# Half of the first product of batches 3 and 5 by Strassen's algorithm, with q^T, x and v in single buffers

## The chip, the cores and the metric

One core of a Trainium2 chip runs the whole kernel. Its engines work side by side, each through a queue of its own in program order: TensorE (PE, with its weight loads listed as PEld), VectorE (DVE), ScalarE (ACT), GpSimd (POOL) and SyncE (SP, which issues most DMAs). The metric is device time in microseconds for one execution, lower is better.

## The reference

Eight batches; each goes through attention with a linear kernel and then through a mixer with two matrix products (S = 576 tokens, model width 512, hidden width 2048):

```python
q_p, k_p = phi(q), phi(k)              # relu(x)*cos(pos), relu(x)*sin(pos): 64 -> 128 features
kv  = einsum('bhsf,bhsd->bhfd', k_p, v);  z = sum_s k_p
x   = (q_p @ kv) / (q_p @ z + 1e-6)    # heads side by side: [8, 576, 512]
u   = x + (x^T @ U @ V)^T              # low rank, 32
out = u + relu(u @ w_ch1) @ w_ch2      # 512 -> 2048 -> 512
```

Inputs and output are float32; the kernel multiplies in bf16 and sums in float32.

## The kernel before

**Tokens.** 512 of a batch's 576 tokens are four chunks of 128; the last 64 (the tail) of two batches of a pair make one more tile of 128 tokens.

**Slots.** The mixer's matmuls are laid out by hand as one list of units, the slots (`lay_all`, line 1029). In order: batch 0 first product (slots 0 to 15) and second (16 to 31); batch 1 first (32 to 47), tails of the pair (`g1_tail`, gt, four slots), second product (14 slots, 52 to 65), `g2_tail` (4); batch 2 first (70 to 85) and second (86 to 99); batch 3 first (100 to 115), gt (116 to 119), second (120 to 133), g2_tail (134 to 137); batch 4 first (138 to 153), second (154 to 167); batch 5 first (168 to 183), gt (184 to 187), second (188 to 201); batch 6 first (202 to 217), second (218 to 231); batch 7 first (`LAST`, 19 slots), second, and the last tails. After each slot's matmuls come the things put beside that slot: `starts[b]` is the first slot of batch b's first product. Every engine gets its instructions in exactly this order (`manual_schedule`), so an instruction that waits holds everything behind it on its engine.

**First product.** `g1_main(b, j)` (line 661) makes one of 16 chunks of the hidden layer: four matmuls of 512 columns into one of three PSUM banks with the tag g (G3), then a relu on ACT into `hid`. For batch 7 alone, `g1_part(b, m, part)` (line 587) does it by Strassen's algorithm in the form with seven products: a group m of four chunks, parts 1 to 7, each four matmuls of 256 columns. It takes sums and differences of blocks of w_ch1 (`w1_form`, line 557, into `sa`) and of u^T (`uT_form`, line 575, into `tb`), made on VectorE. Parts 1, 6, 5, 3 add up in one bank (al), each read by ACT before the next is added: three casts into `pw`/`py`, one relu. Parts 2 and 7 open banks (be), part 4 adds to 7's; for each, VectorE adds (line 637) and takes the relu (line 634).

**Second product.** From batch 1 on, `w_part(b, n)` (line 819) does it by the same algorithm: seven steps of two slots each, with differences of hid from `hid_form` (S, line 806; half 0 beside the first product, half 1 beside the second) and of w_ch2 (T). Step 0 goes to bank T, steps 1 to 3 open the three banks g, steps 4 to 6 add to these. ACT casts step 0 into `w_sum`; VectorE adds step 1 to it; POOL makes three adds from it (o_sb, line 850); VectorE makes the other adds of line 850. `store` writes o_sb.

**Attention beside it.** `attention_plan(b)` (line 1054) puts batch b's attention beside the products of the two batches before: features `q_prep`, `k_prep` (line 295 on ACT, 297 on VectorE), casts of v by POOL (`v_prep`), transposes by DMA from SP (`qtr_dma`), then `kv_pair` (line 344; 40 matmuls into bank X, the cast on VectorE), five `x_unit` (line 418; eight matmuls, then add, reciprocal and multiply on VectorE: lines 415, 416, 435), `A_unit` (line 457), `u_va` (line 464), `u_add` (line 484), `u_tail`, and u's transposes by DMA (`utr_dma`). The x_units take banks O and X in turns, each of two PSUM banks. `split_o` (line 261) turns O into two single banks, oA and oB, for batch 7's first product.

Of the kernel before, what the change touches and what calls it, by code (L numbers as in the profile page):

```python
# [17 lines left out]
def kernel(  # L18
# [13 lines left out]
    B = 8  # L32
# [150 lines left out]
    v_ext = [const.tile([P, 5, H, E], BF16, name=f"v_ext{i}") for i in range(2)]  # L183
# [8 lines left out]
    v_tl = const.tile([P, H, E], BF16)  # L192
    V_.memset(v_tl[:, :, D:E], 1.0)
    for i in range(2):
        V_.memset(v_ext[i][:, 0:4, :, D:E], 1.0)
# [15 lines left out]
    V_nat = const.tile([R, S], BF16)  # L211
    four = const.tile([R, P], BF16)
# [3 lines left out]
    for i in range(2):  # L216
        G_.memset(v_ext[i][:, 4, :, :], 0.0)
        G_.memset(v_ext[i][tail(i), 4, :, D:E], 1.0)
# [60 lines left out]

    def v_prep(b, h0=0, h1=H, cs=range(5), engs=None):  # L280
        vx = v_ext[b % 2]
        for n, c in enumerate(cs):
            eng = engs[n] if engs else G_
            if eng is None:
                continue
            if c < 4:
                cast(eng, vx[:, c, h0:h1, 0:D], vst[:, h0:h1, c, :])
            elif b < 2:
                cast(eng, v_tl[:, h0:h1, 0:D], vst[:, h0:h1, 4, :])
            else:  # L290
                cast(eng, vx[tail(b), 4, h0:h1, 0:D], vst[tail(b), h0:h1, 4, :])
# [31 lines left out]
    def kv_unit(b, hg, tag, bufs, eng=None):  # L323
        if b not in kv_sb:
            kv_sb[b] = pool.tile([P, H, E], BF16, tag="kv", bufs=2, name="kv")
        n = D if b == 0 else E
        acc = bank([P, 4, n], FP32, tag, bufs, "kv_ps")
        vx = v_ext[b % 2]
        for i in range(4):
            h = hg * 4 + i  # L330
            for c in range(5):
                nc.tensor.matmul(  # L332
                    out=acc[:, i, :],
                    lhsT=k_p[b][:, c, h, :] if c < 4 else k_tl[:, h, :],
                    rhs=(
                        v0[:, h, c, :] if b == 0
                        else v_tl[:, h, :] if c == 4 and b < 2 else vx[:, c, h, :]
                    ),
                    start=(c == 0),
                    stop=(c == 4),  # L340
                )
        cast(eng or V_, kv_sb[b][:, hg * 4 : hg * 4 + 4, 0:n], acc)

    def kv_pair(b, tag, bufs):
        kv_sb[b] = pool.tile([P, H, E], BF16, tag="kv", bufs=2, name="kv")
        acc = bank([P, 2, 512], FP32, tag, bufs, "kv_ps")
        vx = v_ext[b % 2]
        for h in range(H):
            g, i = divmod(h, 4)
            for c in range(5):  # L350
                nc.tensor.matmul(  # L351
                    out=acc[:, g, i * E : i * E + E],
                    lhsT=k_p[b][:, c, h, :] if c < 4 else k_tl[:, h, :],
                    rhs=vx[:, c, h, :], start=(c == 0), stop=(c == 4),
                )
# [108 lines left out]
    def u_va(b, *parts):  # L464
# [3 lines left out]
        for d0, tag, bufs in parts:  # L468
            t = bank([P, 2, 512], FP32, tag, bufs, "va_ps")
            for i in range(2):  # L470
                va[d0 + i] = t[:, i, :]
            va[d0, "pair"] = t
        for c in range(4):
            for d0, _, _ in parts:
# [6 lines left out]
        for d0, _, _ in parts:  # L481
            va_ps[b, d0] = va[d0, "pair"]

    def u_add(b, d0):
        nc.vector.tensor_tensor(  # L485
            out=u_bf[b][:, d0 : d0 + 2],
            in0=x_bf[b].rearrange("p c (d n) -> p d c n", n=P)[:, d0 : d0 + 2],
            in1=va_ps[b, d0].rearrange("p d (c n) -> p d c n", n=P), op=ALU.add,
        )
# [85 lines left out]
    def uT_form(b, n, tag):  # L575
        if b not in tb:
            tb[b] = pool.tile([P, 4, 2, 256], BF16, tag=tag, bufs=1, name="tb")
# [9 lines left out]
    def g1_part(b, m, part):  # L587
        if b not in hid:
            hid[b] = pool.tile([P, NJ, 512], BF16, tag="hid", bufs=1, name="hid")
        if b not in pw:  # L590
            pw[b] = (
                pool.tile([P, 4, 512], FP32, tag="k_p", bufs=1, name="pw"),
                pool.tile([P, 2, 512], FP32, tag="q_p", bufs=1, name="py"),
            )
        ks = slice(2 * m, 2 * m + 2)
        hf, k0 = divmod(2 * m, 4)

        def s_of(n):
            return sa[hf][:, n, :, k0 : k0 + 2, :]
# [17 lines left out]
        for k_ in range(2):  # L617
# [6 lines left out]
        e = m % 2  # L624
        p_, w_, y_ = (
            t_.rearrange("p (k n) -> p k n", k=2)
            for t_ in (pw[b][0][:, 2 * e], pw[b][0][:, 2 * e + 1], pw[b][1][:, e])
# [56 lines left out]
    def g1_tail(pr, jq):  # L684
        if pr not in hid_tl:
            tag, bufs = ("q_pT", 2) if pr == NPAIR - 1 else ("hid_tl", 1)
# [60 lines left out]
    def g2_tail(pr, part):  # L747
        if part == 0:
            o_ps[pr] = bank([P, DM], FP32, *T1, "ot_ps")
# [15 lines left out]

    HD = DM // 2
# [122 lines left out]
    def tl_form(n):  # L889
        if "s" not in tl:  # L890
            tl["s"] = pool.tile([P, 4, KB, P], BF16, tag="q_pT", bufs=2, name="s_tl")
# [19 lines left out]
    def tl_part(step):  # L911
# [12 lines left out]
        if opens:  # L924
            if step == 0:
                tl["o"] = pool.tile([P, 2, DM], FP32, tag="x_bf", bufs=2, name="o_t2")
# [121 lines left out]

    QORD = (4, 0, 1, 2, 3)
# [4 lines left out]
    def attention_plan(b):  # L1054
# [22 lines left out]
        else:  # L1077
# [14 lines left out]
            kv_at, a_at = X0, x_at[4] + 2  # L1092
            u_at = a_at + 1
            a_bank = T1
# [13 lines left out]
        if odd:  # L1108
            put(u_at + 1, u_tail, *T1)
# [277 lines left out]
```

## Time and profile before

| | us |
|---|---|
| runs | 293.81, 294.84, 294.84 (median 294.84) |
| the profiled execution, its own time | 294.04 |
| its span, first to last instruction | 292.2 |
| TensorE busy | 285.7 (98%) |
| VectorE, ScalarE, GpSimd busy | 209.2, 158.1, 74.1 |
| batch 2 second product | 112.8 to 125.1 |
| batch 3 first product | 125.1 to 142.3 |
| batch 5 first product | 191.5 to 208.7 |
| batch 5 second product | 212.3 to 226 |
| batch 7 first product | 254.6 to 270.5 |

In a row of a timeline stand the start, the length, the engine, the line, the operation, output and inputs, shapes and count, and in brackets how long the engine stood idle before it and what ended that. In the chain, a row is start, length, engine, output, line and count. A matmul is shown with its way through the array, so rows overlap; what one costs is read from the start of one to the start of the next.

### The profile page before, as it was taken

Reading aid. Unit: us, or ns where it says so; the run is one execution under the profiler, and the core shown is the slowest. Engines: PE = TensorE matmul, PEld = TensorE weight load, DVE = VectorE, ACT = ScalarE, POOL = GpSimd, SP = SyncE. Lnnn points to the kernel's source line nnn. Section 1 sums busy time; section 2 is a strip of 40 time slices with the busy share of each in tenths; the row PEclk is TensorE's granted clock in tenths of the full one; section 3 lists DMA queues with packets and bytes.
Section 4 is the critical chain, followed back from the end, with each engine's and each line's share of the span. In section 5 each row is a group of like instructions: output and inputs, shape, how many; then the busy total and the mean of one; then the engine's idle time right before and its main releaser. Section 6 shows DMA issues by size and latency. Waiting matters only on the chain.

```text
span 292.2 us, 7236 instructions
## 1 busy us (share of the span) xinstructions
PE 285.7 (98%) x2990; PEld 201.1 (69%) x3018; DVE 209.2 (72%) x406; ACT 158.1 (54%) x274; POOL 74.1 (25%) x111
## 2 busy tenths in 40 slices
PE   8999999999999999999999999999999999999995
PEld 6776455545987546865787546865698548899884
DVE  4889748887894568747744477547779587969884
ACT  2855651575593466845694356936693552067100
POOL 8350600040053304650042500550033002400220
PEclk9999999999999999999999999999999999999999
DMA  6999999999999997699998916999292304030023
GB/s 196 356 247 252 276 205 263 279 172 166 287 225 155 249 350 156 183 260 217 279 201 187 353 54 128 223 238 298 42 152 52 136 6 86 12 134 4 2 84 132
DMA packets 85444, 53.31 MB, mean 182 GB/s; under 512 B 53988, under 2 KB 83076, under 8 KB 85412
## 3 DMA queue, kind: packets, MB, share of 16 engines
q1 hardware_dynamic: 78996, 41.62, 61.9%
q0 software_dynamic: 6272, 11.17, 15.5%
q8 instruction: 23, 0.38, 0.5%
q14 instruction: 9, 0.07, 0.1%
q10 hardware_dynamic: 144, 0.07, 0.1%
HBM read 36.86 MB, written 9.44 MB: 158 GB/s over the span
## 4 chain that ended last, share of the span: by engine, by line
PE 94%; DMA 3%; DVE 1%; issue 1%; ACT 0%; DVEq 0%; ACTq 0%
PE g_ps L671 33%; PE w_ps L838 29%; PE gt_ps L692 5%; PE o_ps L732 5%; PE x_ps L425 3%; DMA kst<-in_k_dram 3%; PE kv_ps L351 3%; PE al_ps L619 2%; PE ot_ps L752 2%; PE ot_ps L939 2%; PE be_ps L619 2%; PE a_ps L451 1%; PE va_ps L476 1%; PE kv_ps L332 1%; PE t_ps L368 1%
## 5 line engine op out<-in xcount | busy, mean ns | idle before, releaser
L671 PE MATMUL g_ps<-uT,w_bf 128*128 128x512 bf16 x428 | 105.5, 380 | 1.0
L680 ACT ACTIVATE hid<-g_ps 128x512 bf16<-128x512 f32 x112 | 66.5, 597 | 69.3 <-PE g_ps L671 44.2
L671 PEld LDWEIGHTS <-w_bf 128*128 128x128 bf16 x448 | 40.1, 98 | 41.4 <-issue 0.2
L850 POOL TENSOR_TENSOR o_sb<-w_sum,u_bf 128x512 f32<-128x512 f32 x21 | 28.3, 1373 | 122.8 <-DVE w_sum L850 122.8
L838 PEld LDWEIGHTS <-hid 128*128 128x128 bf16 x448 | 43.6, 98 | 5.6
L838 PEld LDWEIGHTS <-S 128*128 128x128 bf16 x336 | 32.6, 98 | 4.0
L838 PE MATMUL w_ps<-T,hid 128*128 128x256 bf16 x224 | 26.9, 273 | 0.0
L838 PE MATMUL w_ps<-w_bf,hid 128*128 128x256 bf16 x224 | 26.9, 273 | 0.0
L850 DVE TENSOR_TENSOR o_sb<-o_sb,w_ps 128x512 f32<-128x512 f32 x28 | 19.1, 683 | 9.8 <-PE w_ps L838 5.2
L838 PE MATMUL w_ps<-T,S 128*128 128x256 bf16 x224 | 25.9, 273 | 0.0
L485 DVE TENSOR_TENSOR u_bf<-x_bf,va_ps 128x1024 bf16<-128x1024 bf16 x16 | 19.3, 1217 | 7.2 <-PE va_ps L476 7.2
L116 POOL CAST v_ext<-vst 128x512 bf16<-128x512 f32 (+1 forms) x30 | 18.9, 667 | 14.1 <-DMA vst<-in_v_dram 13.7
L415 DVE TENSOR_SCALAR rec<-x_ps 128x8 f32<-128x8 f32 (+1 forms) x35 | 5.8, 164 | 20.0 <-PE x_ps L425 19.9
L435 DVE TENSOR_TENSOR x_bf<-x_ps,rec 128x512 bf16<-128x512 f32 x28 | 19.4, 692 | 1.0
L295 ACT ACTIVATE k_p<-kst,sinw 128x512 bf16<-128x512 f32 x26 | 17.1, 711 | 0.7 <-DMA kst<-in_k_dram 0.7
L706 POOL DMA_DIRECT2D out_dram<-o_sb x12 | 7.6, 631 | 38.7 <-DVE o_sb L740 21.8
L692 PE MATMUL gt_ps<-uT_tl,w_bf 128*128 128x128 bf16 x256 | 15.8, 219 | 0.0
L692 PEld LDWEIGHTS <-w_bf 128*128 128x128 bf16 x256 | 14.9, 98 | 0.8
L732 PE MATMUL o_ps<-w_bf,hid 128*128 128x512 bf16 x61 | 15.3, 380 | 0.2
L116 DVE CAST kv<-kv_ps 128x520 bf16<-128x520 f32 (+1 forms) x8 | 5.1, 632 | 14.1 <-PE kv_ps L351 9.0
L425 PEld LDWEIGHTS <-q_pT 128*128 128x128 bf16 x224 | 10.8, 98 | 5.9
L295 ACT ACTIVATE q_p<-qst,cosw 128x512 bf16<-128x512 f32 x21 | 14.4, 711 | 0.1
(187 smaller groups left out, 431.7 us busy)
## 6 DMA issues: line engine op xcount, KB each, us to landing
qst<-in_q_dram SPq DMA_DIRECT2D x14, 512.0 KB, 6.4
kst<-in_k_dram SPq DMA_DIRECT2D x14, 512.0 KB, 8.7
vst<-in_v_dram SPq DMA_DIRECT2D x12, 512.0 KB, 8.1
out_dram<-o_sb POOLq DMA_DIRECT2D x12, 512.0 KB, 6.7
w_bf<-in_moe_w_ch_dram POOLq DMA_DIRECT2D x8, 512.0 KB, 10.0
out_dram<-o_sb SPq DMA_DIRECT2D x4, 512.0 KB, 3.0
qst<-in_q_dram SPq DMA_DIRECT2D x2, 640.0 KB
kst<-in_k_dram SPq DMA_DIRECT2D x2, 640.0 KB, 11.0
```

Of the source, the lines that this page charges most:

```text
L116: eng.tensor_copy(out=o, in_=i)
L295: nc.scalar.activation(out=o, in_=i, func=AF.Relu, bias=0.0, scale=w)
L425: nc.tensor.matmul(out=acc[:, g, i * E : i * E + E], lhsT=qT_of(b, c, h), rhs=kv_sb[b][:, h, :], start=True, stop=True,)
L435: nc.vector.tensor_tensor(out=x_of(b, c, rows).rearrange("p (g i d) -> p g i d", g=2, d=D), in0=view[:, :, :, 0:D], in1=rec[rows].unsqueez ...
L485: nc.vector.tensor_tensor(out=u_bf[b][:, d0 : d0 + 2], in0=x_bf[b].rearrange("p c (d n) -> p d c n", n=P)[:, d0 : d0 + 2], in1=va_ps[b, d0 ...
L619: nc.tensor.matmul(out=res[:, k_, :], lhsT=lhs[:, d, k_, :], rhs=rhs[:, d, :], start=(opens and k_ == 0 and d == 0), stop=(k_ == 1 and d = ...
L671: nc.tensor.matmul(out=g_ps.rearrange("p (c t) -> p c t", c=4), lhsT=w1_bf[:, d, j * P : j * P + P], rhs=uT[b][:, d, :, :], start=(d == 0) ...
L680: nc.scalar.activation(out=hid[b][:, j, :], in_=g_ps, func=AF.Relu, bias=0.0, scale=1.0)
L692: nc.tensor.matmul(out=g_ps[:, jj, :], lhsT=w1_bf[:, d, j * P : j * P + P], rhs=uT_tl[pr][:, d, :], start=(d == 0), stop=(d == 3),)
L732: nc.tensor.matmul(out=o, lhsT=hid[0][:, j, cc * P : cc * P + P], rhs=w2_bf[:, j, :], start=(j == 0), stop=(j == NJ - 1),)
L838: nc.tensor.matmul(out=res[:, g, :], lhsT=lhs[:, k_, g * P : g * P + P], rhs=rhs[:, k_, :], start=(opens and k_ == 0 and g == 0), stop=(k_ ...
L850: eng.tensor_tensor(out=o, in0=x, in1=y, op=ALU.add)
```

## The change

Batches 3 and 5 (`MIXED`) do groups 0 and 2 of the four by Strassen's algorithm, their parts laid between the whole chunks of groups 1 and 3 (`HALF`; s4 is chunk 4m + 4). Group m = 0 takes slots 0 to 7 of the stage, m = 2 slots 8 to 15. The banks: al in T, part 2 in g, part 7 in oA.

The sums of w_ch1 for groups 0 and 2 move from batch 5's second product to batch 2's, in a buffer of their own (`sa`); those for groups 1 and 3 stay in batch 6's; each operation covers one group (512 elements, two operations in place of one of 1024). The four `uT_form` of batches 3 and 5 come beside the last four slots before their first products. `split_o` moves from batch 6's end to slot 98, so from batch 4 on the x_units have X alone, A_unit takes oB, u_va takes X and oA, oB (with u_add in three pieces), and u_tail takes half of X two slots later. Batches 4 and 6 get kv_pair one slot later and x_units at slots 5, 8, 13, 16, 18 of the stage in place of 3, 5, 7, 9, 11; their u follows. The first halves of hid_form in batches 3 and 5 move from slots 8 to 11 to slots 9, 11, 17, 18. From batch 4 on ACT makes kv's cast. q_pT, x_bf and the four main chunks of v are held once, not twice; several tiles take other tags. On SP, the tail's q transpose of batch 7 goes ahead of u's first transpose of batch 6, and u^T's second half of batches 5 and 7 ahead of the tail's by more.

```diff
@@ v and its tails
-    v_ext = [const.tile([P, 5, H, E], BF16, name=f"v_ext{i}") for i in range(2)]
+    v_ext = const.tile([P, 4, H, E], BF16)
+    v_ext_tl = [const.tile([P, H, E], BF16, name=f"v_ext_tl{i}") for i in range(2)]
...
@@ kv_pair
         cast(
-            V_, kv_sb[b].rearrange("p (g i) e -> p g (i e)", g=2), acc[:, :, 0 : 4 * E]
+            A_ if b > 3 else V_, kv_sb[b].rearrange("p (g i) e -> p g (i e)", g=2),
+            acc[:, :, 0 : 4 * E],
         )
...
-            q_pT[b] = pool.tile([P, 4, H, P], BF16, tag="q_pT", bufs=2, name="q_pT")
+            q_pT[b] = pool.tile([P, 4, H, P], BF16, tag="q_pT", bufs=1, name="q_pT")
...
-            x_bf[b] = pool.tile([P, 4, DM], BF16, tag="x_bf", bufs=2, name="x_bf")
+            x_bf[b] = pool.tile([P, 4, DM], BF16, tag="x_bf", bufs=1, name="x_bf")
...
@@ w1_form
-    def w1_form(n, hf, tag):
-        if hf not in sa:
-            sa[hf] = pool.tile([P, 4, 2, 4, P], BF16, tag=tag, bufs=1, name=f"sa{hf}")
-        t = sa[hf]
-        ks = slice(4 * hf, 4 * hf + 4)
+    def w1_form(n, m):
+        if m % 2 not in sa:
+            tag = ("sa", "qst")[m % 2]
+            sa[m % 2] = pool.tile([P, 2, 4, 2, 2, P], BF16, tag=tag, bufs=1, name="sa")
+        t = sa[m % 2][:, m // 2]
+        ks = slice(2 * m, 2 * m + 2)
...
@@ g1_part
         if part == 1:
-            g_al[b, m] = bank([P, DM], FP32, *(OA, OB, T1)[m % 3], "al_ps")
+            g_al[b, m] = bank([P, DM], FP32, *((OA, OB, T1)[m % 3] if last else T1), "al_ps")
         elif part in (2, 7):
-            g_be[b, m, part] = bank([P, DM], FP32, *(X1S if part == 2 else G3), "be_ps")
+            tg = (X1S, G3) if last else (G3, OA)
+            g_be[b, m, part] = bank([P, DM], FP32, *tg[part == 7], "be_ps")
...
+    MIXED = {3: (0, 2), 5: (0, 2)}
...
+    HALF = ("1", "s4", "6 2", "s5", "5 7", "s6", "3", "s7 4")
+
     def first_units(b):
         starts[b] = len(slots)
-        lay([lambda j=j: g1_main(b, j) for j in range(NJ)], False)
+
+        def unit(names, m):
+            def go():
+                for n in names:
+                    if n[0] == "s":
+                        g1_main(b, 4 * m + int(n[1]))
+                    else:
+                        g1_part(b, m, int(n))
+
+            return go
+
+        for m in (0, 2):
+            if m in MIXED.get(b, ()):
+                lay([unit(n.split(), m) for n in HALF], False)
+            else:
+                lay([lambda j=j: g1_main(b, j) for j in range(4 * m, 4 * m + 8)], False)
         for i in range(4 * (0 < b)):
-            beside.setdefault(starts[b] + (12 + 2 * i if b == 1 else 8 + i), []).append(
+            n = 12 + 2 * i if b == 1 else (9, 11, 17, 18)[i] if b in MIXED else 8 + i
+            beside.setdefault(starts[b] + n, []).append(
                 lambda i=i: hid_form(b, (1, 2, 4, 3)[i], 0)
             )
...
@@ attention_plan
-            kv_at, a_at = X0, x_at[4] + 2
+            kv_at = X0
+            if b in (4, 6):
+                kv_at, x_at = G + 1, [G + i for i in (5, 8, 13, 16, 18)]
...
+            a_at = x_at[4] + 2
             u_at = a_at + 1
-            a_bank = T1
+            a_bank = T1 if b == 3 else OB
...
-            put(x_at[n], x_unit, c, *(O1, X1)[n % 2])
+            put(x_at[n], x_unit, c, *((O1, X1)[n % 2] if b < 4 else X1))
         put(a_at, A_unit, *a_bank, A_)
-        put(u_at, u_va, (0, *X1), (2, *O1))
+        put(u_at, u_va, (0, *X1), (2, *O1) if b < 4 else (2, OA, OB))
...
-            put(u_at + 1, u_tail, *T1)
+            put(*((u_at + 1, u_tail, *T1) if b < 4 else (u_at + 3, u_tail, *X1S)))
...
-        put(starts[B - 3] + 21 + 2 * n, lambda n=n: w1_form(n, 0, "vst"))
-        put(s6 + 17 + 2 * n, lambda n=n: w1_form(n, 1, "qst"))
-        put(s6 + 24 + n, lambda n=n: uT_form(B - 1, n, "kst"))
+        for m in (0, 2):
+            put(starts[2] + 17 + 2 * n, lambda n=n, m=m: w1_form(n, m))
+            put(s6 + 17 + 2 * n, lambda n=n, m=m: w1_form(n, m + 1))
+        for b in MIXED:
+            put(starts[b] - 4 + n, lambda b=b, n=n: uT_form(b, n))
+        put(s6 + 24 + n, lambda n=n: uT_form(B - 1, n))
...
-    put(s6 + 24, split_o)
+    put(starts[3] - 2, split_o)
```

More of the change, by code (lines that the diff above doesn't have):

```diff
@@ L191 @@
     A_sb = [const.tile([P, P], BF16, name=f"A_sb{i}") for i in range(3)]
-    v_tl = const.tile([P, H, E], BF16)
+    v_tl = pool.tile([P, H, E], BF16, tag="w_sum", bufs=1, name="v_tl")
     V_.memset(v_tl[:, :, D:E], 1.0)
-    for i in range(2):
-        V_.memset(v_ext[i][:, 0:4, :, D:E], 1.0)
+    V_.memset(v_ext[:, :, :, D:E], 1.0)
     V_.memset(q_tlT, 0.0)
@@ L216 @@
     for i in range(2):
-        G_.memset(v_ext[i][:, 4, :, :], 0.0)
-        G_.memset(v_ext[i][tail(i), 4, :, D:E], 1.0)
+        G_.memset(v_ext_tl[i], 0.0)
+        G_.memset(v_ext_tl[i][tail(i), :, D:E], 1.0)
     def cast_uv():
@@ L467, in u_va @@
         va = {}
-        for d0, tag, bufs in parts:
-            t = bank([P, 2, 512], FP32, tag, bufs, "va_ps")
+        for d0, *tags in parts:
+            if tags[0] in (OA, OB):
+                t = [bank([P, 512], FP32, *tg, "va_ps") for tg in tags]
+                va[d0, "pair"] = [x[:, None, :] for x in t]
+            else:
+                x = bank([P, 2, 512], FP32, *tags, "va_ps")
+                t = [x[:, i, :] for i in range(2)]
+                va[d0, "pair"] = [x]
             for i in range(2):
-                va[d0 + i] = t[:, i, :]
-            va[d0, "pair"] = t
+                va[d0 + i] = t[i]
         for c in range(4):
-            for d0, _, _ in parts:
+            for d0, *_ in parts:
                 for d in (d0, d0 + 1):
@@ L480, in u_va @@
                     )
-        for d0, _, _ in parts:
+        for d0, *_ in parts:
             va_ps[b, d0] = va[d0, "pair"]
     def u_add(b, d0):
[L485 to L489, printed above, removed]
+        for t in va_ps[b, d0]:
+            n = t.shape[1]
+            nc.vector.tensor_tensor(
+                out=u_bf[b][:, d0 : d0 + n],
+                in0=x_bf[b].rearrange("p c (d n) -> p d c n", n=P)[:, d0 : d0 + n],
+                in1=t.rearrange("p d (c n) -> p d c n", n=P), op=ALU.add,
+            )
+            d0 += n
     def u_tail(b, tag, bufs):
@@ L623, in g1_part @@
                 )
-        e = m % 2
         p_, w_, y_ = (
-            t_.rearrange("p (k n) -> p k n", k=2)
-            for t_ in (pw[b][0][:, 2 * e], pw[b][0][:, 2 * e + 1], pw[b][1][:, e])
+            pw[b][m % 2 if last else 0][:, i].rearrange("p (k n) -> p k n", k=2)
+            for i in range(3)
         )
@@ L685, in g1_tail @@
         if pr not in hid_tl:
-            tag, bufs = ("q_pT", 2) if pr == NPAIR - 1 else ("hid_tl", 1)
+            tag, bufs = ("kst", 1) if pr == NPAIR - 1 else ("hid_tl", 1)
             hid_tl[pr] = pool.tile([P, NJ, P], BF16, tag=tag, bufs=bufs, name="hid_tl")
@@ L1047 @@
     lay_all()
+    ODDX = (5, 8, 11, 13, 15)
     QORD = (4, 0, 1, 2, 3)
```

47 lines of the change are left out of this document (24 added, 23 removed).

## The prediction

> **What bounds the kernel now.** Four views, in this order. The page's busy rows come first:
>
> ```profile
> PE 285.7 (98%) x2990; PEld 201.1 (69%) x3018; DVE 209.2 (72%) x406; ACT 158.1 (54%) x274; POOL 74.1 (25%) x111
> PEclk9999999999999999999999999999999999999999
> PE 94%; DMA 3%; DVE 1%; issue 1%; ACT 0%; DVEq 0%; ACTq 0%
> ```
>
> TensorE is busy 98% of the span at a full granted clock and is 94% of the chain that ended last. The waits of TensorE alone are two, 1.2 and 0.3 us, both in the first 13 us. So a matmul taken out is worth its own time, and any wait put in front of TensorE is paid in full. Next, what a matmul costs, from the chain in order of time:
>
> ```profile
> 97.46 1.73 PE g_ps L671 x8
> ...
> 259.50 1.31 PE al_ps L619 x12
> ```
>
> A 512-column matmul of a whole chunk advances TensorE by 0.216 us, a 256-column matmul of a Strassen part by 0.109 us, its weight load included. Third, how full VectorE is, stage by stage, from the table of windows (columns: window, length, then PE, PEld, DVE, ACT, POOL):
>
> ```profile
> 96.30:112.80 16.50, 16.40 (x149) 8.10 (x149) 11.38 (x23) 9.12 (x16) 3.00 (x5) 1.00 1.03 299
> 112.80:125.10 12.30, 12.30 (x114) 10.86 (x112) 9.72 (x16) 9.76 (x16) 8.20 (x8) 1.00 0.68 153
> 125.10:142.30 17.20, 16.99 (x179) 9.18 (x182) 9.90 (x22) 9.12 (x16) 3.52 (x6) 1.00 1.04 243
> ```
>
> These are batch 2's first product, batch 2's second product, batch 3's first product. In the middle one VectorE works 9.7 of 12.3 us and POOL, at 8.2 us, is busier than anywhere else. Last, VectorE's timeline there:
>
> ```profile
> 114.22 0.99 DVE L806 TENSOR_TENSOR S<-S,hid 128x1024 bf16<-128x1024 bf16 x1
> 115.14 0.83 DVE L297 TENSOR_SCALAR q_tl<-qst,sinw 64x512 bf16<-64x512 f32 x1
> 115.89 0.82 DVE L297 TENSOR_SCALAR q_p<-qst,sinw 128x512 bf16<-128x512 f32 x1
> ...
> 118.05 0.67 DVE L850 TENSOR_TENSOR w_sum<-w_sum,w_ps 128x512 f32<-128x512 f32 x1
> 118.64 0.67 DVE L806 TENSOR_TENSOR S<-hid,S 128x1024 bf16<-128x1024 bf16 x1
> 120.37 1.48 DVE L850 TENSOR_TENSOR o_sb<-o_sb,w_ps 128x512 f32<-128x512 f32 x2 [1.05 <-POOL o_sb L850]
> ...
> 124.03 0.88 DVE L297 TENSOR_SCALAR k_p<-kst,cosw 128x512 bf16<-128x512 f32 x2
> ```
>
> The last k_p ends at 124.91, and kv_pair of batch 4, which needs it, starts on TensorE at 125.76: 0.85 us of slack. An operation whose operands all lie in SBUF stretches while POOL works: 0.99 for 0.69, 0.83 for 0.48. Batch 6 shows it plainly, VectorE's row first and POOL's (line 850, alone 1.12 to 1.16) after it:
>
> ```profile
> 217.13 1.65 DVE L806 TENSOR_TENSOR S<-hid,S 128x1024 bf16<-128x1024 bf16 x1
> ...
> 216.69 1.53 POOL L850 TENSOR_TENSOR o_sb<-w_sum,u_bf 128x512 f32<-128x512 f32 x1 [20.46 <-DVE w_sum L850]
> ```
>
> S waits until POOL's add ends at 218.2 and then runs some 0.55 us: the two take turns. The adds that read PSUM (w_sum, o_sb) keep 0.67 to 0.69 beside POOL.
>
> **The change, part by part.** *Saved on TensorE.* A group of four chunks costs 16 x 0.216 = 3.46 us whole and 28 x 0.109 = 3.06 us in seven parts; four groups save 4 x 0.40 = 1.6 us. No other matmul goes.
>
> *VectorE in batch 2's second product.* Eight w1_form operations on 512 elements come in, two after each of slots 87, 89, 91, 93, and the four uT_form of batch 3 after slots 96 to 99, each ahead of the k_p feature of its slot. A row for 512 bf16 elements is tb at 0.415 us, 0.34 from start to start (252.88 to 253.21). Other steps from start to start: a form of S 0.60, a feature 0.40, an add 0.60. I walk the new queue from 115.89, where the first pair follows q_tl. While POOL casts v (114.06 to 117.85) each turn is shared: the pair ends at 117.5, then q_p 117.9, the hid form 118.5, q_p 118.9, w_sum 119.5 (before 118.7). Now come pair, S, add, pair, add, pair, add, tb, k_p, add, tb, k_p, tb, k_p: 3 x 0.68 + 0.60 + 4 x 0.60 + 3 x 0.34 + 3 x 0.40 = 7.3 us without POOL, so 126.8. But w_sum releases POOL's three adds, 3 x 1.1 us, in that very stretch; taking turns costs 1.8 us if VectorE goes first whenever two of its operations follow each other, 2.4 us if POOL does (in the rows after 115.2 POOL went first three times of four). The last k_p ends at 128.6 to 129.2.
>
> TensorE wants kv_pair(4) one slot later than before: 124.89 (first matmul of the stage) + 0.44 (part 1) + 0.86 (chunk 4) = 126.2. The wait is 2.4 to 3.0 us; I take 2.8. A part of it shows earlier: part 1 needs bank T, which the third add of the walk releases near 126, 1 us after 124.9. Bounds: 0 if no operation meets POOL (the whole queue then ends at 125.1, from 113.50 by the same steps), 0.6 if only the casts are met, 3.5 if each turn is lost. Behind the wait nothing else is late: VectorE has 10.6 us of work in the 15 us of batch 3's first product (six adds of 0.68, six relus of 0.29, three x_units of 1.1, two S), and catches up.
>
> *Batch 5's end.* Features of batch 7 on VectorE (slots 184 to 186), two S forms and x_units of batch 6 (184, 186) now meet in the four gt slots, 3.6 us + 2 x 0.25. From the last part's end: add and relu 1.05, x_unit to 2.4, feature 2.8, S 3.4, feature 3.8, hid 4.4, x_unit 5.5. A_unit's last four matmuls want that x at 4.06 + 0.87 + 0.31 = 5.25: 0.3 us of wait. Bounds 0 and 1.1 (POOL in the way once). At batch 3 there are no features in those slots: x at 4.7, no wait.
>
> *At nothing, and what covers it.* (1) ACT: three casts and a relu of 0.60 take the place of four relus of 0.60 per group; part 6 follows part 1 by 0.87 us or more while the cast takes 0.2 + 0.60, a margin near zero without the x_unit or kv_pair that lies there (0.25, 1.2 us); if it goes, under 0.1 us a time. (2) kv casts from VectorE to ACT: 0.6 us, ACT idle after its features (2.78 us idle at 126.0). (3) Bank X alone for x_units: one is held 1.6 us (matmuls at 97.04, multiply done 98.63) and the next comes after 1.98; cover 0.4 us, and a late VectorE operation would cost its excess. (4) Single q_pT, x_bf and v_ext: each writer comes after its last reader in slot order, the closest being q_pT of batch 7 (slot 189 after 186). (5) SP: uT of batch 6 is issued behind the q_pT transposes of batch 7 (1.6 to 2.2 us each) at 12.9 us after the last part, lands 4.3 later (median of its rows; 6.8 at most) at 17.2, wanted at 18.6 to 19.0; cover 1.8, cost 0.7 at worst. The tail's uT moves two slots later and is wanted 12 slots on. (6) w1_form in batch 6's second product: eight of 0.34 for four of 0.60, and POOL's turns make VectorE some 1.9 us later at 254.7; there it stood idle 2.5 us until 259.35 (wait of hid for py), which absorbs it. (7) u_add in three pieces: 0.1 us. (8) One memset less, at a start that waits 8.75 us for kst.
>
> *Sum.* -1.6 + 2.8 + 0.3 = +1.5 us. The profiled execution took 294.04 us (span 292.2), so 295.5. The three shown runs are 293.81 and twice 294.84; the profiled execution is 0.8 under their median, and I carry half of that: 296.0.
>
> **A rule against the change.** Weight loads per group rise from 16 to 28 at 98 ns each. In the last batch, where the whole product is in parts, 112 such matmuls advance by 0.109 us each with PEld busy 14.59 of 15.90 us, so the loads hide. Exposed, the 48 extra loads of the four groups would cost 4.7 us. The Trainium skill (TensorE: Matmul & The Clock Gate, The mechanism) says that weight loads overlap running matmuls only when they use other rows of the array, which these do not; by it the sum would be +6.2 us. The trace does not bear it out in the last batch, so the sum goes by the row.
>
> **The rivals.** *Faster: VectorE's backlog never reaches TensorE.* For it: the queue without POOL ends at 125.1, a microsecond before the need, and S at 118.64 kept 0.67 us because it began ahead of POOL's add. Against it: eight new operations just where w_sum lets POOL go. It decides when the last k_p is done by 126.2. Then 294.04 - 1.6 + 0 to 0.3, some 292.6, and 293.0 with the carry; a wait of 0.6 gives 293.6.
> *Slower still: the crowding at batch 5's end also holds TensorE.* POOL once in the way (1.1), uT late (0.7), banks X waiting for VectorE (0.4 each at two or three units): 1 to 2.5 us more, 297 to 298.5. For it: all margins there are under 2 us. Against it: the same stage had 1.79 us of VectorE idle and loses four w1_form of 0.69 to 1.05.
> *The halved matmuls save nothing:* if the weight loads do not hide where whole chunks alternate with parts, 48 x 0.098 = 4.7 us come on top: 300.7. For it: PEld is already at 69%. Against it: the last batch's 0.109 us. The page named above would have it so.
>
> **How the numbers follow.** Forecast 0.52, slower still 0.22, faster rival 0.22 (half of it a partial wait that leaves no measurable gain), nothing saved 0.02, others 0.02 (half on each side). About 0.5%, 1.5 us, is what a measurement can tell from no change. The forecast's own range, 0.9 to 2.0 us over its base, lies across that border, so it is split: 0.28 same, 0.24 slower. Same: 0.28 + 0.11 = 0.39. Slower: 0.24 + 0.22 + 0.02 + 0.01 = 0.49. Faster: 0.11 + 0.01 = 0.12. The forecast's own range is 295.2 to 296.8; the range for 8 in 10 runs from the faster rival with a small wait, 293.2, to slower still, 298.0.
>
> **What would show each step.** In the changed profile: the parts of batches 3 and 5 (line 619 before) advancing 0.109 us a matmul; a TensorE wait of about 1 us before the first al_ps of batch 3, ended by VectorE's o_sb, and one of about 1.7 before kv_ps, ended by VectorE's k_p; w_sum of batch 2 near 119.5 and the last k_p near 129; sa at 0.42 when POOL is idle and near 1 when not. At batch 5's end a 0.3 us wait of a_ps for x_bf. The chain should show DVE at 2% where it had 1%. No wait before kv_ps means the faster rival; waits before va_ps, x_ps or batch 6's g_ps mean the slower one.

## The result, and the profile after

The changed kernel takes 295.57 us (median of 16 runs, 294.84 to 296.78) where the kernel before, run beside it, took 294.31 us (16 runs, 293.54 to 296.36): a ratio of 1.004, 95% interval 1.0023 to 1.0057. It is slower by 1.3 us as the medians stand (0.7 to 1.7 by the interval), about what the forecast of 296.0 had (+1.5 over the profiled execution). The profiled execution of the changed kernel took 294.84 us (span 293.0), the fastest of its runs, so the traces differ by 0.8 us only. 0.25 us of that gap lies at the start: batch 1's tails begin at 73.75 us here and at 74.00 before. The start varies by more than this between kernels that share its code (73.5 to 75.2 us in the traces below), so the stages are compared by their lengths. From batch 1's tails to the first `tl_part` the kernel before takes 208.55 us and the changed one 209.59: +1.04 us, inside the interval.

The page's busy rows and the head of its chain:

```profile
PE 285.0 (97%) x3040; PEld 206.1 (70%) x3066; DVE 219.5 (75%) x445; ACT 160.1 (55%) x278; POOL 73.4 (25%) x111
PE 91%; DVE 3%; issue 3%; POOL 2%; ACT 0%; DVEq 0%; POOLq 0%
```

TensorE's share of the chain falls from 94% to 91%; VectorE and POOL, which had 1% and none, have 3% and 2%. More than half of POOL's share is its casts of v (2.65 us), which the chain reaches through 2.98 us of "issue"; TensorE waits for none of them directly. The waits of TensorE say where (us in total, times, longest):

```profile
PE w_ps L202 <- DVE zero L125: 1.2, 1, 1.2
PE kv_ps L350 <- DVE k_p L301: 0.7, 2, 0.5
PE w_ps L848 <- DVE o_sb L860: 0.7, 1, 0.7
PE a_ps L451 <- DVE x_bf L435: 0.4, 1, 0.4
```

The first is that of the start, as before. The other three are new: before kv_pair, before a step of the second product, and before A_unit's last matmuls. These rows count the idle time alone; what TensorE loses is read from start to start. Its timeline shows the places:

```profile
119.55 1.91 PE L848 MATMUL w_ps<-w_bf,hid 128*128 128x256 bf16 x16
121.59 1.91 PE L848 MATMUL w_ps<-w_bf,S 128*128 128x256 bf16 x16
124.17 1.91 PE L848 MATMUL w_ps<-T,hid 128*128 128x256 bf16 x16 [0.67 <-DVE o_sb L860]
125.91 0.60 PE L629 MATMUL al_ps<-uT,w_bf 128*128 128x256 bf16 x4
...
127.59 0.19 PE L350 MATMUL kv_ps<-v_ext,k_p 128*128 128x65 bf16 x1 [0.16 <-DVE k_p L301]
128.32 0.19 PE L350 MATMUL kv_ps<-v_ext,k_p 128*128 128x65 bf16 x1 [0.54 <-DVE k_p L301]
...
146.98 0.24 PE L451 MATMUL a_ps<-x_tl,U_bf 128*32 128x128 bf16 x4
...
147.38 1.05 PE L848 MATMUL w_ps<-w_bf,hid 128*128 128x256 bf16 x8
...
212.62 0.24 PE L451 MATMUL a_ps<-x_tl,U_bf 128*32 128x128 bf16 x4
...
213.38 0.24 PE L451 MATMUL a_ps<-x_bf,U_bf 128*32 128x128 bf16 x4 [0.35 <-DVE x_bf L435]
213.56 1.05 PE L848 MATMUL w_ps<-w_bf,hid 128*128 128x256 bf16 x8
```

A step of 16 matmuls goes on after 1.75 us when nothing holds it. Step 5 starts 2.04 us after step 4, and step 6 starts 2.58 us after step 5; step 6 writes the bank of step 3, which VectorE reads in the add that ends at 124.12. Step 5's 0.29 us too much are the same kind of wait: it writes the bank of step 2, read by the add that ends at 121.54. So TensorE is held before the stage ends, and not at bank T, where the forecast put it. Bank T came free at 125.38, in time for part 1 at 125.91 only because steps 5 and 6 had been held: without them part 1 was due at 124.80. A_unit (from 212.62) takes 0.94 us to the next step's matmuls in batch 5, where it takes 0.40 in batch 3 (146.98 to 147.38): its wait costs 0.54 us.

VectorE's timeline of the changed kernel in this stretch:

```profile
114.13 0.98 DVE L816 TENSOR_TENSOR S<-S,hid 128x1024 bf16<-128x1024 bf16 x1
...
115.79 0.74 DVE L577 TENSOR_TENSOR sa<-w_bf 128x512 bf16<-128x512 bf16 x2
...
117.84 0.68 DVE L860 TENSOR_TENSOR w_sum<-w_sum,w_ps 128x512 f32<-128x512 f32 x1
118.44 0.75 DVE L577 TENSOR_TENSOR sa<-sa,w_bf 128x512 bf16<-128x512 bf16 x2
119.11 0.68 DVE L816 TENSOR_TENSOR S<-hid,S 128x1024 bf16<-128x1024 bf16 x1
120.85 0.69 DVE L860 TENSOR_TENSOR o_sb<-o_sb,w_ps 128x512 f32<-128x512 f32 x1 [1.06 <-POOL o_sb L860]
121.45 2.06 DVE L577 TENSOR_TENSOR sa<-w_bf 128x512 bf16<-128x512 bf16 x2
123.44 0.68 DVE L860 TENSOR_TENSOR o_sb<-o_sb,w_ps 128x512 f32<-128x512 f32 x1
124.04 0.75 DVE L577 TENSOR_TENSOR sa<-w_bf,sa 128x512 bf16<-128x512 bf16 x2
...
127.70 0.47 DVE L301 TENSOR_SCALAR k_p<-kst,cosw 128x512 bf16<-128x512 f32 x1
```

And POOL's, the three adds that it makes from w_sum in one row; behind it the first of the three as the chain has it:

```profile
118.61 4.63 POOL L860 TENSOR_TENSOR o_sb<-w_sum,u_bf 128x512 f32<-128x512 f32 x3 [3.02 <-DVE w_sum L860]
```

```profile
118.61 2.22 POOL o_sb L860
```

A pair of forms takes 0.75 us, except the one at 121.45, which takes 2.06: it lies beside POOL's adds until 123.24. The add behind it, which frees step 3's bank, comes that much later. The pair at 118.44 and S at 119.11 kept their time, and there POOL paid: its first add took 2.22 us, alone 1.12 to 1.16, and VectorE's next add stood idle for it. The queue's last k_p ends at 128.17; before it ended at 124.91.

The account by stage, from one stage's first matmul to the next one's:

| stage | before | after | difference | what it holds |
|---|---|---|---|---|
| batch 2 second product | 12.22 | 13.49 | +1.27 | waits for o_sb +1.13; steps 1 and 2 +0.14 |
| batch 3 first product | 17.26 | 16.02 | -1.24 | parts -0.80; x_units -0.51 and A_unit with u_va -0.93, moved out; wait for k_p +1.0 |
| its gt, and second product | 15.80 | 17.25 | +1.45 | x_units +0.52, A_unit with u_va +0.93 |
| batch 5 first product | 17.25 | 15.01 | -2.24 | as at batch 3, without a wait |
| its gt, and second product | 17.19 | 19.00 | +1.81 | as at batch 3, A_unit's wait +0.54, and -0.18 at batch 7's kv_pair, which took 1.39 before and takes 1.20 |

From batch 1's tails on, the other stages agree within 0.03 us. Saved are 1.60 us at the parts and 0.18 at kv_pair, lost 1.27 + 1.0 + 0.54 = 2.81: +1.03 us.

### The profile page after: what moved, and what is told of

Its sections match the earlier page's. It is cut to its first block, busy times and chain, and to the rows that moved or that the text cites. A ratio compares the mean times of both kernels' runs of the same rounds, so it can differ in the third digit from the quotient of the medians.

```text
span 293.0 us, 7400 instructions
## 1 busy us (share of the span) xinstructions
PE 285.0 (97%) x3040; PEld 206.1 (70%) x3066; DVE 219.5 (75%) x445; ACT 160.1 (55%) x278; POOL 73.4 (25%) x111
## 3 DMA queue, kind: packets, MB, share of 16 engines
q0 software_dynamic: 6272, 11.17, 15.8%
## 4 chain that ended last, share of the span: by engine, by line
PE 91%; DVE 3%; issue 3%; POOL 2%; ACT 0%; DVEq 0%; POOLq 0%
PE g_ps L680 28%; PE w_ps L848 25%; PE o_ps L741 5%; PE al_ps L629 5%; PE gt_ps L701 4%; PE be_ps L629 4%; PE w_ps L202 3%; PE x_ps L425 3%; PE kv_ps L350 2%; PE ot_ps L761 2%; PE ot_ps L949 2%; PE a_ps L451 1%; PE va_ps L481 1%; POOL v_ext L116 1%; PE kv_ps L335 1%
## 5 line engine op out<-in xcount | busy, mean ns | idle before, releaser
L680 PE MATMUL g_ps<-uT,w_bf 128*128 128x512 bf16 x366 | 90.7, 379 | 0.8
L689 ACT ACTIVATE hid<-g_ps 128x512 bf16<-128x512 f32 x96 | 57.0, 597 | 47.1 <-PE g_ps L680 38.7
L680 PEld LDWEIGHTS <-w_bf 128*128 128x128 bf16 x384 | 34.8, 98 | 34.3 <-issue 0.2
L114 ACT ACTIVATE pw<-al_ps 128x512 f32<-128x512 f32 x24 | 14.2, 596 | 19.4 <-PE al_ps L629 18.7
L646 DVE TENSOR_TENSOR hid<-pw,be_ps 128x512 bf16<-128x512 f32 x24 | 16.4, 684 | 10.5 <-PE be_ps L629 5.8
L492 DVE TENSOR_TENSOR u_bf<-x_bf,va_ps 128x1024 bf16<-128x1024 bf16 (+1 forms) x20 | 19.6, 1003 | 4.2 <-PE va_ps L481 4.2
L701 PE MATMUL gt_ps<-uT_tl,w_bf 128*128 128x128 bf16 x256 | 16.4, 219 | 0.0
L116 POOL CAST v_ext<-vst 128x512 bf16<-128x512 f32 x24 | 15.6, 691 | 2.4 <-DMA vst<-in_v_dram 2.1
L701 PEld LDWEIGHTS <-w_bf 128*128 128x128 bf16 x256 | 15.0, 98 | 0.4
```

What stands on the lines that cost most here:

```text
L116: eng.tensor_copy(out=o, in_=i)
L492: nc.vector.tensor_tensor(out=u_bf[b][:, d0 : d0 + n], in0=x_bf[b].rearrange("p c (d n) -> p d c n", n=P)[:, d0 : d0 + n], in1=t.rearrange ...
L646: V_.tensor_tensor(out=o, in0=x, in1=res, op=ALU.add)
L680: nc.tensor.matmul(out=g_ps.rearrange("p (c t) -> p c t", c=4), lhsT=w1_bf[:, d, j * P : j * P + P], rhs=uT[b][:, d, :, :], start=(d == 0) ...
L689: nc.scalar.activation(out=hid[b][:, j, :], in_=g_ps, func=AF.Relu, bias=0.0, scale=1.0)
L701: nc.tensor.matmul(out=g_ps[:, jj, :], lhsT=w1_bf[:, d, j * P : j * P + P], rhs=uT_tl[pr][:, d, :], start=(d == 0), stop=(d == 3),)
```

## The experiments

The theory: the forms of w_ch1 and u^T put VectorE's queue late at the border from batch 2 to batch 3, POOL's turns make it later, and TensorE pays about 2.3 us there; the parts save 1.6 us in any case. Rivals: the loss is elsewhere (single buffers, the moved x_units, ACT's casts), or the parts save less than it seems. Differences from the changed kernel are worked out from the two ratios to the kernel before, since not all ran on one chip; beside them stand, where they say more, the lengths of stages in the one trace of each kernel.

**The forms of w_ch1 some 24 us earlier.** They go beside batch 1's tails, where VectorE has idle time and POOL makes no adds.

```diff
-            put(starts[2] + 17 + 2 * n, lambda n=n, m=m: w1_form(n, m))
+            put(starts[2] - 4 + n // 2, lambda n=n, m=m: w1_form(n, m))
```

> The eight sums of w_ch1 for groups 0 and 2 are made beside slots 66 and 67, when VectorE has little to do and POOL nothing, in place of slots 87 to 93. Queue theory (these eight, lengthened by turns with POOL, made VectorE late; TensorE paid 1.3 us before the last step of batch 2's second product and 1.0 before kv_pair): batch 2's second product goes back from 13.5 to 12.2 us on TensorE, the wait before kv_pair to under 0.2, and the time falls by 2.1 to 2.3 us against the changed kernel, to about 0.997 of the kernel before. Rival (the loss lies in the stages with parts, in banks and alternation, and in the attention that was moved): under 0.5 us is gained, and the ratio stays near 1.003.

Measured: 292.95 us (12 runs, 292.5 to 293.59), ratio to before 0.9952 (0.9931 to 0.9973). Against the changed kernel that is 0.9952 / 1.004 = 0.991, some 2.6 us less (1.8 to 3.4). This kernel's VectorE rows, the forms in their new place and the last k_p:

```profile
91.93 0.75 DVE L577 TENSOR_TENSOR sa<-w_bf 128x512 bf16<-128x512 bf16 x2
92.60 0.75 DVE L577 TENSOR_TENSOR sa<-sa,w_bf 128x512 bf16<-128x512 bf16 x2
93.27 0.75 DVE L577 TENSOR_TENSOR sa<-w_bf 128x512 bf16<-128x512 bf16 x2
93.94 0.75 DVE L577 TENSOR_TENSOR sa<-w_bf,sa 128x512 bf16<-128x512 bf16 x2
...
124.84 0.48 DVE L301 TENSOR_SCALAR k_p<-kst,cosw 128x512 bf16<-128x512 f32 x1
```

Of its TensorE waits only A_unit's is left of the three:

```profile
PE a_ps L451 <- DVE x_bf L435: 0.4, 1, 0.4
```

All pairs take 0.75 us and the last k_p ends at 125.32, 13.1 us after batch 2's second product began (112.21), where it was 15.8 us. Batch 2's second product is down to 12.43 us and batch 3's first to 15.01, as long as batch 5's. So the place of the forms holds 2.1 of the 2.3 us lost at that border, and with them moved the change is worth 1.4 us (0.8 to 2.0) against the kernel before, 1.0 by the lengths from batch 1's tails on.

**The same without parts.** Forms and attention stay where this kernel puts them, but batches 3 and 5 multiply whole chunks. With `MIXED` empty, three more things of the change go: both batches' uT_form are not made, the sums of w_ch1 for groups 0 and 2 only serve batch 7, and hid_form is back at its old slots.

```diff
-    MIXED = {3: (0, 2), 5: (0, 2)}
+    MIXED = {}
```

> As the run with early forms, but batches 3 and 5 make their first product in whole chunks: all of the change but the parts themselves (single buffers, banks, moved x_units, kv casts on ACT, early sums). If the parts save what the matmul rows say, this run is 1.6 us slower than the one with early forms, and 0.3 to 0.7 us slower than the kernel before (A_unit and u_va between parts of the second product cost some 0.2 us more a batch). Rival (parts between whole chunks save less, since banks and ACT hold them): the difference is under 0.8 us.

Measured, on the chip of the last run: 294.28 us (12 runs, 293.43 to 295.5), ratio 0.9988 (0.9964 to 1.0011). It is 1.33 us slower than the kernel with the parts; that one also has A_unit's wait of 0.54, which this one, with hid_form back at its old slots, has not, so 1.60 - 0.54 = 1.06 was due. By stage it is plainer: batches 3 and 5 take 15.79 us each here and 15.01 and 15.00 there. The parts save 0.78 us a batch. The expectation of a time above the kernel before by some tenths was a miss: single buffers, ACT's casts and the moved x_units together cost nothing that can be measured. The rivals on them fall; that hid_form's new slots cost A_unit's wait this run can't tell from the parts.

**Without POOL's adds, first try.** Batch 2's three adds on POOL are left out and ACT copies w_sum to o_sb at step 1 instead.

```diff
-            add(G_, by_d(o1[:, :, hi]), by_d(w), u(2, 1))
-            add(G_, by_d(o0[:, :, hi]), by_d(w), u(0, 1))
-            add(G_, by_d(o1[:, :, lo]), by_d(w), u(2, 0))
+            if b == 2:
+                for o in (o1[:, :, hi], o0[:, :, hi], o1[:, :, lo]):
+                    cast(A_, o, w)
+            else:
+                ...
```

> The changed kernel, but in batch 2 alone POOL's three adds of w_sum and u are left out: ACT copies w_sum into the three places, so u is missing there. VectorE has all its operations as before. If turns with POOL make the backlog: sa in that stage takes 0.42 us each and never 1 us, the last k_p ends some 2 us earlier (near 126), and the time falls by 1.8 to 2.3 us against the changed kernel. Rival (there are simply too many operations for VectorE, POOL or not): the last k_p ends within 0.7 us of the changed kernel's, and the time falls by less than 0.7 us.

Measured: 294.39 us (10 runs, 293.5 to 295.77), ratio 0.9991 (0.9963 to 1.0019), some 1.4 us less than the changed kernel, not the 2.3 of the whole border. The wait for o_sb is gone, but this kernel's TensorE waits have a new row:

```profile
PE kv_ps L350 <- ACT k_p L299: 1.1, 3, 0.4
```

The copies wait for w_sum at the head of ACT's queue, and ACT's own k_p features behind them became the last. VectorE's own last k_p came 13.97 us after the stage began (15.76 in the changed kernel), as expected without POOL's turns. But the run replaced one late queue by another, so its time decides nothing.

**Without POOL's adds, the copies late.** The same again, but each copy stands just ahead of the add that needs it.

```diff
+        if b == 2 and step in (2, 5, 6):
+            r, cs = {2: (1, hi), 5: (0, hi), 6: (1, lo)}[step]
+            cast(A_, o_alloc(b, r)[:, :, cs], w_sum[b])
...
-            add(G_, by_d(o1[:, :, hi]), by_d(w), u(2, 1))
+            if b != 2:
+                add(G_, by_d(o1[:, :, hi]), by_d(w), u(2, 1))
...
```

> As the run without POOL's adds in batch 2 (u is missing in the same three places), with ACT's three copies put where ACT reaches them only once w_sum is there and its own features are not held up: before the adds of steps 2, 5 and 6. If turns with POOL are what made VectorE late, nothing else takes their place now: the last k_p of either engine ends by 126.3, no wait before the last step of batch 2's second product, at most 0.5 us before kv_pair, and 1.7 to 2.3 us less than the changed kernel. Rival (VectorE has too many operations with or without POOL): less than 0.7 us.

Measured: 293.48 us (12 runs, 292.76 to 294.71), ratio 0.9947 (0.9921 to 0.9973), some 2.7 us less than the changed kernel (1.8 to 3.6); the two stages at the border together are 1.95 us shorter. This kernel's VectorE rows, where every form is still in its place:

```profile
119.25 0.74 DVE L577 TENSOR_TENSOR sa<-sa,w_bf 128x512 bf16<-128x512 bf16 x2
119.92 0.67 DVE L816 TENSOR_TENSOR S<-hid,S 128x1024 bf16<-128x1024 bf16 x1
120.52 0.67 DVE L860 TENSOR_TENSOR o_sb<-o_sb,w_ps 128x512 f32<-128x512 f32 x1
121.12 0.74 DVE L577 TENSOR_TENSOR sa<-w_bf 128x512 bf16<-128x512 bf16 x2
...
126.06 0.47 DVE L301 TENSOR_SCALAR k_p<-kst,cosw 128x512 bf16<-128x512 f32 x1
```

The pair takes 0.74 us in place of 2.06, and the add ahead of it no longer stands 1.06 us idle for POOL's first sum. The last k_p ends 13.8 us after the stage began (112.72), 1.9 us sooner than in the changed kernel, and no wait at the border is left. So the new operations fit when POOL does no adds. The run takes away two things at once: the pair's lost turn, 2.06 - 0.74 = 1.3 us, and the idle time for POOL's first sum, which the kernel before had too (1.05). The run doesn't part them, but the changed kernel's rows do in part: step 5 was held by the add that waited for POOL's first sum (0.29 us), step 6 by the add behind the pair (0.83 us).

**The forms of u^T later.** Only batch 3's uT_form move behind the features; the forms of w_ch1 stay crowded.

```diff
-            put(starts[b] - 4 + n, lambda b=b, n=n: uT_form(b, n))
+            at_ = (starts[b] - 1 + (0, 0, 1, 2)[n]) if b == 3 else starts[b] - 4 + n
+            put(at_, lambda b=b, n=n: uT_form(b, n))
```

> The changed kernel with batch 3's four uT_form behind the k_p features (slots 99, 99, 100, 101 in place of 96 to 99); the sums of w_ch1 stay in batch 2's second product. If TensorE's wait at this border has two causes in one queue, the sums of w_ch1 and the differences of u^T, then the last k_p ends some 1.0 us earlier (near 127.2), the wait before kv_pair falls from 1.0 to under 0.2, and the wait of 1.3 us before the last step of batch 2's second product stays: 0.8 to 1.0 us faster than the changed kernel. Rival (the sums of w_ch1 alone matter): less than 0.3 us is gained.

Measured: 294.92 us (12 runs, 294.23 to 295.66), ratio 0.9993 (0.9968 to 1.0017): 1.4 us less than the changed kernel (0.5 to 2.3), the profiled spans 0.5 us. Its TensorE waits:

```profile
PE w_ps L848 <- DVE o_sb L860: 1.2, 2, 0.7
PE a_ps L451 <- DVE x_bf L435: 0.4, 1, 0.4
```

The wait for k_p is gone, that for o_sb is not: batch 2's second product takes 13.92 us and batch 3's first 15.21. The wait for o_sb grew by 0.43 us (POOL's casts and with them w_sum came later in the stage: w_sum was done 6.53 us after its start, 6.10 in the changed kernel), so the two stages together gain 0.37 us only, where 0.8 to 1.0 was expected. The pairs among the adds alone make the banks late. For k_p to be late it takes both, the pairs and the uT_form: the first experiment moved only the pairs, this one only the uT_form, and in either the wait is gone.

**Batch 5's end: x_units earlier.** From here on each kernel has the early forms of the first experiment; against that kernel's 292.95 us and its A_unit wait (0.35 us idle, 0.54 from start to start, as in the changed kernel) they are read. First, x_units of batches 4 and 6 close up, so that VectorE has the last x done sooner.

```diff
-                kv_at, x_at = G + 1, [G + i for i in (5, 8, 13, 16, 18)]
+                kv_at, x_at = G + 1, [G + i for i in (5, 8, 11, 13, 15)]
```

> As the run with early forms, with batch 4's and 6's x_units at slots 5, 8, 11, 13, 15 in place of 5, 8, 13, 16, 18, so that A_unit falls into the gt slots and not behind the first slot of the second product. Queue theory: the 0.35 us wait of A_unit for x_bf at batch 5's end goes, and A_unit and u_va no longer stand between parts (0.2 us each batch): 0.3 to 0.8 us faster than the run with early forms. Rival (VectorE is as full inside the stage with parts as behind it): a wait of 0.3 us or more appears there, before a part or an x_unit, and the time stays within 0.3 us.

Measured: 293.26 us (12 runs, 292.73 to 294.35), ratio 0.996 (0.994 to 0.998), on the chip of the first experiment. A_unit's wait is gone, but small ones came (0.2 us before a step of the second product, for S, among them) and the time is the same within what these runs can tell. The lengths say why: from batch 5's first product to batch 6's it takes 33.74 us where early forms takes 34.00, but from batch 3's to batch 4's 37.19 where that takes 36.93. What is gained at one is paid at the other.

**Batch 5's end: features later.** Batch 7's features on VectorE go from the gt slots to slots 189 to 191.

```diff
-                for eng in (A_, V_)[: 1 + (s_ in ((0, 1, 2, 10, 11, 12) if b > 3 else (1, 2, 10, 11, 12)))]:
+                for eng in (A_, V_)[: 1 + (s_ in ((5, 6, 7, 10, 11, 12) if b == 7 else (0, 1, 2, 10, 11, 12) if b > 3 else (1, 2, 10, 11, 12)))]:
```

> As the run with early forms, with batch 7's three q features on VectorE at slots 189 to 191 in place of 184 to 186. If these features are what makes batch 6's last x_unit late for A_unit, the wait of A_unit of 0.37 us goes and nothing takes its place: 0.3 to 0.4 us faster than early forms, which the profile shows more plainly than the times. Rival (S forms and x_units alone fill the gt slots): the wait of A_unit stays above 0.2 us, or one of the same size comes before va_ps or a later part.

Measured: 294.31 us (12 runs, 292.9 to 295.57), ratio 0.9962 (0.9935 to 0.9988), no gain over 0.9952. A_unit's wait is gone. This kernel's VectorE in batch 5's second product:

```profile
218.20 1.41 DVE L301 TENSOR_SCALAR k_tl<-kst,cosw 64x512 bf16<-64x512 f32 x1
219.64 1.53 DVE L816 TENSOR_TENSOR S<-hid,S 128x1024 bf16<-128x1024 bf16 x1
221.10 0.68 DVE L860 TENSOR_TENSOR o_sb<-o_sb,w_ps 128x512 f32<-128x512 f32 x1
```

And the TensorE row that waits for it:

```profile
221.83 1.36 PE L848 MATMUL w_ps<-w_bf,S 128*128 128x256 bf16 x11 [1.01 <-DVE o_sb L860]
```

Work moved out of the full slots met POOL's adds (217.06 to 220.63) and made a bank late by 1.0 us: the trap of the change itself, now in batch 5's second product.

**Batch 4 by parts as well.** On top of the last, groups 0 and 2 of batch 4 go by parts. Of batch 5's attention, which stands beside them, A_unit and u come five slots later; kv_pair and the x_units keep their slots, two apart, since the two lines that would have moved them go.

```diff
-    MIXED = {3: (0, 2), 5: (0, 2)}
+    MIXED = {3: (0, 2), 4: (0, 2), 5: (0, 2)}
...
-            elif b - 1 in MIXED:
-                kv_at, x_at = G + 1, [G + i for i in ODDX]
-            a_at = x_at[4] + 2
+            a_at = x_at[4] + (7 if b == 5 else 2)
```

> As the run with later features, with batch 4 mixed too (groups 0 and 2 in parts, its uT_form beside slots 134 to 137, batch 5's A_unit and u after slots 153 and 154). The parts save 0.80 us more if VectorE has room: 0.5 to 0.8 us faster than the run with later features. Rival (batch 4's second product, without gt or g2_tail slots to catch up in, gets two S forms, u_add and the features together, and VectorE is late again): waits of 0.5 us or more before w_ps, kv_ps or a part of batch 5, and no gain.

Measured: 296.34 us (12 runs, 295.36 to 298.02), ratio 1.0046 (1.002 to 1.0073). Its two largest TensorE waits:

```profile
PE w_ps L848 <- DVE o_sb L860: 2.2, 2, 1.2
PE x_ps L425 <- DVE x_bf L435: 1.4, 2, 1.1
```

And one row of VectorE's timeline in batch 4's first product:

```profile
166.24 1.28 DVE L643 TENSOR_SCALAR hid<-hid 128x512 bf16<-128x512 bf16 x1
```

Here bank X alone for the x_units does hold TensorE (1.4 us), after a relu that takes 1.28 us, beside POOL's casts of v, where it takes 0.29 elsewhere; how much of it the x_units' old slots make the run doesn't show. Of the waits for o_sb the one of 1.2 us is new, in batch 4's second product; the other is that of the last run. On the same chip it is 2.0 us slower than the kernel it is built on, where the parts of a third batch were to save 0.8.

**One S form later.** On top of the early forms, the third of the four hid_form moves from slot 17 to slot 24 of the stage.

```diff
-            n = 12 + 2 * i if b == 1 else (9, 11, 17, 18)[i] if b in MIXED else 8 + i
+            n = 12 + 2 * i if b == 1 else (9, 11, 24, 18)[i] if b in MIXED else 8 + i
```

> As the run with early forms, with the first half of S4 in batches 3 and 5 seven slots later (offset 24 in place of 17: behind w_sum in the second product). It takes 0.6 us out of VectorE's queue ahead of batch 6's last x_unit. If that queue is a plain sum, the wait of A_unit of 0.37 us goes, and the steps of the second product, which later features could not be fitted into, hold since one operation of 0.6 to 1.5 us still ends before step 5: 0.2 to 0.4 us faster than early forms. Rival: the operation meets POOL's adds, and a wait of 0.5 us or more comes before step 5 or 6.

Measured: 293.09 us (8 runs, 292.06 to 294.58), ratio 0.9928 (0.9892 to 0.9964). A_unit's wait is gone and one before a step of the second product came in its place. It is the lowest ratio of all, but its interval overlaps that of the early forms alone; both beat the kernel before. The lengths part the two: from batch 5's first product to batch 6's it takes 33.46 us (34.00 with early forms), from batch 3's to batch 4's 37.26 (36.93), where the moved form met POOL's adds and took 1.65 us. So A_unit's wait is worth its 0.54 us where nothing takes its place, as at batch 5 here; as a gain in the time none of the three runs shows it.

## Why the prediction was right

*Saved on TensorE, 1.6 us:* right. Batch 5's first product, once what moved out of it is taken off, is 0.80 us shorter, and the run without parts shows 0.78 us a batch. The parts advance by 0.109 us a matmul between whole chunks too (in the chain, parts 6 and 2 of batch 3's first group take 0.44 us for four matmuls each, the whole chunk behind them 0.22 us a matmul). The rule weighed against the change, weight loads showing (Trainium skill, TensorE: Matmul & The Clock Gate, The mechanism), is not borne out here either: 4.7 us of loads would have left no saving to find. The same section names a second case, a load into a background weight buffer; the runs don't show which case this is.

*VectorE in batch 2's second product, a wait of 2.8 us:* the mechanism was right and the term over-sized. 1.27 + 1.0 = 2.27 us is below its own 2.4 to 3.0. 0.14 us of it lies in steps 1 and 2 and has another cause, which the kernel with early forms shows too (0.21): the S that step 1's second half needs, stretched beside POOL's casts of v, was done at 115.11, 2.69 us after the stage began (2.54 before), and that half was due after one and a half steps, 2.62. Two steps of the walk failed. It let the first pair and three operations behind it share turns with POOL's casts; but the casts began at 112.38, 1.7 us earlier than before (114.06), and were over at 115.59, so w_sum was done at 118.52, not 119.5. That is luck more than reckoning: POOL waits there for v's transfer, and in the kernels of the experiments the casts begin anywhere from 0.07 us ahead of the stage's start to 1.04 behind it. And beside POOL's three adds only one pair lost its turn, 1.3 us, where 1.8 to 2.4 were counted. Against that the walk left out the 1.05 us in which the o_sb add stands idle for POOL's first sum, though the row was shown. These last two errors cancel, by luck: 1.3 + 1.06 = 2.4 us. The last k_p ended at 128.17, where 128.6 to 129.2 was forecast.

*Its place:* half right. The wait for k_p before kv_pair came (1.0 us, forecast 1.7). The part said to show earlier, at bank T before part 1, did not: TensorE was held in the two steps before it, at the banks that steps 5 and 6 add to while VectorE has not read the sums of steps 2 and 3 out of them. Bank T would have held part 1 all the same (free at 125.38, due at 124.80); the earlier waits covered it. I had looked at who opens a new bank and not at who adds to an old one.

*Batch 5's end, 0.3 us:* the wait came where it was said and is 0.54 us from start to start. The last x was done 5.76 us after the first gt matmul began, forecast 5.5 after the last part's end.

*At nothing:* the list held. None of ACT's casts, bank X alone, the single buffers, uT of batch 6 on SP or the forms in batch 6's second product shows a wait in the changed kernel, and the run without parts, which keeps nearly all of them, stands at 0.9988 of the kernel before. That bank X alone is thin fits its 0.4 us of cover: batch 4 by parts, with the x_units two slots apart, made it wait.

*The sum* was +1.5 us on the profiled execution; by the traces it is +0.8, by the lengths of the stages +1.04, by the medians +1.3. Worked out with the measured terms, -1.60 + 2.27 + 0.54 = +1.21, and batch 7's kv_pair, which the list had not, gives 0.18 back. The wait came out smaller than forecast and A_unit's larger, so the total is nearer than its terms. The rival without a wait, 292.6 to 293.0, is what the same change gives with its forms elsewhere: 292.95.

## What to carry to other kernels

Work that an algorithm saves on the bound engine comes back as preparation on another: price the slot where the preparation is put, by that engine's queue and by what its neighbours do just there, not by its average share; here eight operations of 0.34 us each decided the sign. Before moving them, list for each accumulation who must read a bank before the next step may add to it, since a late queue is paid at the first such bank and not only at the consumer of the new data. An experiment that empties a full stretch needs the same look at the stretch it fills.

## What the runs showed of the hardware

VectorE's operations that lie wholly in SBUF waited for the end of POOL instructions: the pair of sums 2.06 us beside POOL's adds and 0.74 to 0.75 without, k_tl 1.41 where such a feature takes 0.47 to 0.49, S 1.53 for 0.68. The adds that read PSUM kept 0.67 to 0.69 beside the same POOL adds. The Trainium skill (GPSIMD Engine Reference, Key points) names contention with VectorE instructions that have two SBUF inputs or use a two-port mode. The rows of the pair and of S, with two inputs in SBUF, agree and give the price, the rest of the POOL instruction under way; whether k_tl and the relu of batch 4, with one, ran in such a mode no run shows. The turn can go the other way: S at 119.11 kept 0.68 us although POOL's add had begun at 118.61, and the pair before it kept 0.75, while that add took 2.22 us in place of 1.15. Someone pays either way; what decides who, the runs don't show.

A_unit with u_va cost TensorE 0.93 us in the first product before and, without a wait, in the second product after, so the kind of matmul around them made no difference.
